# Retention and a squared-ReLU feed-forward on one core: q of the first four pairs read in 2 KB rows, and a new order on every engine

## The chip, the cores and the metric

The kernel runs on one core of a Trainium2 chip. Its time is the device time of one execution in microseconds; the time of a kernel is the median of its runs. Of one execution the profiler also left a trace: every instruction of TensorE (PE for matmuls, PEld for weight loads), VectorE (DVE), ScalarE (ACT) and GpSimd (POOL), the issues of SyncE (SP), and every packet of the 16 DMA engines.

## The reference

Eight batches, eight heads, 576 tokens, head dimension 64; then a feed-forward of 512 to 2048 to 512 over the 4608 tokens.

```python
def _attn_ref(q, k, v):
    scores = scale * np.matmul(q, k.transpose(0, 1, 3, 2))
    gamma = 1.0 - 2.0 ** (-5.0 - np.arange(H))
    rel = pos[:, None] - pos[None, :]
    Dmat = np.where(rel >= 0, gamma[:, None, None] ** rel[None, :, :], 0.0)
    return np.matmul(scores * Dmat[None], v)
...
    x = attn_out.transpose(0, 2, 1, 3).reshape(B * S, H * D)
    h = x @ w_in
    r = np.maximum(h, 0.0)
    return (r * r) @ w_out
```

## The kernel before

**Units, pairs, groups.** A unit is 128 tokens of one batch with all heads (36 in all; the last 64 tokens of two batches share a tail unit). Two units form a group g, 18 groups. The first eight units are loaded as four pairs of 256 tokens (`add_load_pair`, L308): k, q and v of a pair are one DMA of 512 KB each, with two neighbouring tokens of a head, 512 bytes, as a row. Later units are loaded one by one (`add_load`, L290), their q in 1 KB rows by four DMAs.

**Retention.** For a pair (`add_unit_pair`, L403), k and q are cast to fp16 into `kx` and `qx` (L424) on the engine that the code names (DVE, ACT or POOL), and v is scaled by its decay into `vx` (L420). TensorE transposes `kx` and `qx` (L439, into `psT`), and ACT or DVE evicts them to `kqT` (L450). Then (`add_ret_pair`, L468) come the scores `psc` (quarter-array matmuls, L357), the causal mask on DVE (L490, into `rx`), the sums `psS` of the state, the state update on DVE (L514, L461, into `R`), the outputs `psO`, and their product with `gam_full` on DVE, which writes the feed-forward's input `xT` (L577). Later units use DMA transposes (L400) and the lines L371, L382, L387, L692 and L751 in place of these.

**Feed-forward.** For each group (`add_ff`, L858), 64 matmuls `ph` (L876) multiply `xT` with `w_in`; ACT takes the ReLU into `rl` (L884), and ACT or DVE squares it into `gT` (L894, L896), eight times per group (fb 0 to 7). Group 0 multiplies `gT` by `w_out` directly (L916, 16 steps of two units). The other groups use one level of Strassen's scheme (`add_strassen`, L932): seven products of eight matmuls (L973) on sums `gS` that DVE makes (L946), and on sums `wT` of `w_out` that DVE makes once (L827). Product 6 needs the sum s2, which DVE makes in two halves of 128 x 512. ACT and DVE then assemble the output (L986, L996, L1047) and SP stores it (L845).

**Weights.** `w_in` and `w_out` are read by eight DMAs that POOL issues (L331) and that write fp16: w0 to w3 are quarters of `w_in`, w4 to w7 of `w_out`. w0 is issued when v of the first pair has landed. k of the third pair (k4) waits for w5.

**What sets the order.** Nothing is issued where the code stands. Every task goes to a small planner (`Schedule`, L16) with its engine, a priority (`key`), a planned duration, its dependencies and the buffers that it takes. `emit` plays the plan through and then issues the instructions engine by engine in that order. Each engine works in order, so the plan's durations and landing times decide what stands behind what. Warm-up matmuls (L256, `WARM` of them) have the lowest priority and fill TensorE while it has nothing else in the plan.

```python
        loaded[name, u] = loaded[name, u + 1] = dma_task(0, 1.81 if loaded else 2.9, fn, acq=("wst",) if name != "q" else (),
                                                         after=2.1 + LAG.get(name + str(u), 0.0))
```

Of the kernel before, what the change touches and what calls it, by code (L numbers as in the profile page):

```python
# [15 lines left out]
class Schedule:  # L16
# [6 lines left out]

    def add(self, eng, key, dur, fn, deps=(), acq=(), after=None, lag=0.0):
        t = dict(eng=eng, key=key, dur=dur, fn=fn, acq=acq, n=len(self.tasks), users=[], free=[], lag=lag,
                 left=len(deps), ready=0.0, lat=self.LAT[eng] if after is None else after)
        for d in deps:
            d["users"].append(t)
        self.tasks.append(t)
        return t  # L30
# [11 lines left out]
    def emit(self):  # L42
# [10 lines left out]
        for t in self.tasks:  # L53
            if t["left"] == 0:
                heapq.heappush(ready[t["eng"]], (t["key"], t["n"], t))
        now = 0.0
        while True:
            for e in ready:
# [3 lines left out]
                while ready[e]:  # L62
                    item = heapq.heappop(ready[e])
                    t = item[2]
                    if all(self.count[r] >= t["acq"].count(r) for r in t["acq"]):
                        for r in t["acq"]:
                            self.count[r] -= 1
                        t["start"] = now
                        order.append(t)
                        busy[e] = True  # L70
                        push(now + t["dur"], "end", t)
                        break
                    held.append(item)
# [5 lines left out]
            while events and events[0][0] <= now + 1e-9:  # L79
                _, _, what, t = heapq.heappop(events)  # L80
                if what == "end":
                    busy[t["eng"]] = False
                    for w in t["users"]:

                        push(now + (0.0 if w["eng"] == t["eng"] else t["lat"]), "dep", w)
# [18 lines left out]
def kernel(  # L104
# [105 lines left out]

    mask2 = const.tile([P, 2, 2, 64], FP32, name="mask2")
    nc.gpsimd.memset(mask2, 1.0)
    for c in range(2):
        for e in range(2):
            m = mask2[c * 64:(c + 1) * 64, e]
            nc.gpsimd.affine_select(out=m, in_=m, compare_op=ALU.is_ge, fill=0.0, base=-e, pattern=[[1, 2], [2, 64]],  # L216
                                    channel_multiplier=-2)
# [6 lines left out]
    L = 2 * NF  # L224
    WARM = 34
    EARLY = 20
    SQ_ACT = (0, 1, 2, 3, 4, 5, 6)
    SPREAD = 0.1
    QL = 0.8
    BESIDE = 1.1  # L230
    PAUSE = 1.5
# [4 lines left out]
    JOIN = 5  # L236
    LAG = {"k4": 0.7, "q4": 0.5}
    LAG_T, LAG_O = 1.5, 5.0
# [69 lines left out]
    def add_load_pair(name, u):  # L308
        n = "kqv".index(name)

        def fn():
# [3 lines left out]
            b, c = units[u][1:]  # L315
            t = nc.sync.dma_start(out=x, in_=(k, q, v)[n][b, :, c * P:(c + 2) * P, :].rearrange("h (p e) d -> p h (e d)", e=2))
            if (name, u) == ("k", 4):
                behind(t, tile_of["w", 5])
            tile_of["load", name, u] = t
        loaded[name, u] = loaded[name, u + 1] = dma_task(0, 1.81 if loaded else 2.9, fn, acq=("wst",) if name != "q" else (),  # L320
                                                         after=2.1 + LAG.get(name + str(u), 0.0))

    issues = []

    def add_weight(i):
# [9 lines left out]
        issues.append(issue)  # L335
        t = add("SP", 0, 2.75, lambda: None, deps=last_load + [issue], after=2.1 + LAG.get(f"w{i}", 0.0))
        last_load[:] = [t]
# [65 lines left out]
    def add_unit_pair(u, base):  # L403
# [4 lines left out]
        for i, name in enumerate("kqv"):  # L408
            xs[name] = []
            for e in range(2):  # L410
                eng = ("DVE" if (e if name == "v" else lead) else "ACT" if name == "k" and u >= 4 or u == 2 and e else
                       "DVE" if name == "q" and u == 2 else "POOL")

                def fc(name=name, e=e, eng=eng):
# [4 lines left out]
                    if name == "v":  # L419
                        (nc.vector if eng == "DVE" else nc.gpsimd).tensor_tensor(  # L420
                            out=t.rearrange("p (h d) -> p h d", d=D), in0=x,
                            in1=vdec[f"pair{e}"].rearrange("p (h o) -> p h o", o=1).to_broadcast([P, H, D]), op=ALU.mult)
                    else:
                        engines[eng](out=t.rearrange("p (n b a d) -> p n b a d", n=2, b=2, a=2),  # L424
# [9 lines left out]
        for i, name in enumerate("kq"):  # L434
# [9 lines left out]
            for s in range(2):  # L444
                on_act = i == 0 or s == 0 or u > 0

                def fe(i=i, s=s, on_act=on_act):
                    if i == 0:
                        tile_of["kqT", u + s] = work.tile([P, 2 * NP, P], FP16, name="kqT", tag="kqT", bufs=6)
                    (nc.scalar.copy if on_act else nc.vector.tensor_copy)(  # L450
                        out=tile_of["kqT", u + s][:, i * NP:(i + 1) * NP].rearrange("p x (e t) -> p e x t", e=2),
                        in_=tile_of["psT", u, i][:, :, :, half(s)])
                es.append(add("ACT" if on_act else "DVE", base + 3 + i + s / 2, 0.66, fe, deps=[t] + T["kqT", u + s],
# [14 lines left out]
    def add_ret_pair(g):  # L468
# [7 lines left out]
        for e in range(2):  # L476
# [11 lines left out]
            for a in range(2):  # L488
                def fm(e=e, a=a):
                    nc.vector.tensor_tensor(  # L490
                        out=rT[e][:, a], in0=rT["ps", e][a].rearrange("p (n i) -> p n i", i=P),
                        in1=mask2[:, e].rearrange("p (o e) i -> p o (e i)", o=1).to_broadcast([P, NP, P]), op=ALU.mult)
                ms.append(add("DVE", base + 5 + e, 0.66, fm, deps=[t] + ms))
# [79 lines left out]
        for s in range(2):  # L573
            def fx(s=s):
                if s == 0:
                    tile_of["x", g] = x_pool.tile([P, NP, 2 * P], FP16, name="xT", tag="xT")
                nc.vector.tensor_tensor(  # L577
                    out=tile_of["x", g][:, :, s * P:(s + 1) * P].rearrange("p n (i e) -> p n e i", e=2),
                    in0=tile_of["psO", g][s].rearrange("p (n e i) -> p n e i", n=NP, e=2),
                    in1=gam_f.rearrange("p n (i e) -> p n e i", e=2), op=ALU.mult)  # L580
            T["x", u + s] = add("DVE", base + 25 + s, 0.7, fx, deps=[t] + ([T["x", u]] if s else []), acq=() if s else ("x",))
# [119 lines left out]
    def after_sums(g, t, key, res):  # L701
# [23 lines left out]
        r1 = add("DVE", key + 0.2 - URGENT, 0.69, fr1, deps=[r0])  # L725
        r2 = add("DVE", key + 0.3, 0.65, fr2, deps=[r1], acq=("R",))
        T["Rm", g], T["R", g], T["Rread", g], T["Rmread", g] = r0, r2, [], r1
# [94 lines left out]
    def add_wT(i, in0, in1):  # L822
        ts = []
        for h in range(2):
            def f(h=h):
                sl = slice(h * HF // 2, (h + 1) * HF // 2)
                nc.vector.tensor_tensor(out=wT[i][:, sl], in0=in0[:, sl], in1=in1[:, sl], op=ALU.subtract)  # L827
            ts.append(add("DVE", WT_KEY + i, 0.7, f, deps=sum((wcast[j] for j in range(4, 8 if i else 6)), [])))
        return ts
# [5 lines left out]
    for x, y in ((t2, t1), (t4, t2)):  # L835
        for p in y:
            for w in x:
                sched.need(w, p)
    wT_done = {7: t3, 6: t2, 5: t1, 4: t4}
# [18 lines left out]
    def add_ff(g):  # L858
# [10 lines left out]
        for fb in range(NF // nf):  # L869
# [18 lines left out]
            def fg(fb=fb, on_act=on_act):  # L888
# [6 lines left out]
                else:  # L895
                    nc.vector.tensor_tensor(out=t, in0=rl, in1=rl, op=ALU.mult)  # L896
            r = add("ACT", place(4 * fb + 4), 0.6, fr, deps=[f1[-1]], acq=("rl",))
            sched.free("ff", [r])
            sq.append(add("ACT" if on_act else "DVE", place(4 * fb + 6), 0.63 if on_act else 0.55, fg, deps=[r] + sq[:1],
                          acq=() if fb else ("g",)))  # L900
            sched.free("rl", [sq[-1]])
# [30 lines left out]
    def add_strassen(g, us, base, sq):  # L932
# [7 lines left out]
        def add_sum(k, key, parts, in0, in1, op, deps, start=()):  # L940
            out_ = []
            for h in range(parts):
                def f(sl=cut(parts, h)):
                    if ("S", g) not in tile_of:
                        tile_of["S", g] = stage.tile([P, 4, HF, P], FP16, name="gS", tag="wst")
                    nc.vector.tensor_tensor(out=tile_of["S", g][:, k, sl], in0=in0(sl), in1=in1(sl), op=op)  # L946
                out_.append(add("DVE", key + h, (BESIDE if h else 0.5) if parts > 1 else 0.8, f, deps=deps(h, parts) + list(start)))
            sums[k] = out_
# [163 lines left out]
```

## Time and profile before

| | us |
|---|---|
| median of 4 runs | 290.83 |
| lowest and highest | 290.15, 292.28 |
| the profiled execution | 289.97 |
| its span | 288.3 |
| TensorE busy | 281.5 |
| ScalarE, VectorE, GpSimd busy | 187.4, 178.7, 86.6 |
| granted TensorE clock | 0.997 |

The profile's times count from the start of the span. Busy time of TensorE includes the warm-up matmuls, and a busy TensorE isn't TensorE at its peak, since matmuls are pipelined. A row of a group gives line, engine, operation, output and inputs, the shape, the count, and the mean time of one.

### The profile page before, as it was taken

Reading aid. Unit: us, or ns where it says so; the run is one execution under the profiler, and the core shown is the slowest. Engines: PE = TensorE matmul, PEld = TensorE weight load, DVE = VectorE, ACT = ScalarE, POOL = GpSimd, SP = SyncE. Lnnn points to the kernel's source line nnn. Section 1 sums busy time; section 2 is a strip of 40 time slices with the busy share of each in tenths; the row PEclk is TensorE's granted clock in tenths of the full one; section 3 lists DMA queues with packets and bytes.
Section 4 is the critical chain, followed back from the end, with each engine's and each line's share of the span. In section 5 each row is a group of like instructions: output and inputs, shape, how many; then the busy total and the mean of one; then the engine's idle time right before and its main releaser. Section 6 shows DMA issues by size and latency. Waiting matters only on the chain.

```text
span 288.3 us, 10135 instructions
## 1 busy us (share of the span) xinstructions
PE 281.5 (98%) x4346; PEld 236.5 (82%) x4346; DVE 178.7 (62%) x341; ACT 187.4 (65%) x363; POOL 86.6 (30%) x124
## 2 busy tenths in 40 slices
PE   7999999999999999999999999999999999999994
PEld 3568767888888888888888888888888888888883
DVE  3772379968466656747656664867665566364632
ACT  4558975667585857657575748675848675847830
POOL 5560035434435242423235151524423100000000
PEclk9999999999999999999999999999999999999998
DMA  7999999999998898989999897969898620102004
GB/s 197 277 208 206 246 280 268 173 241 152 196 229 175 216 201 212 173 209 175 213 172 234 196 211 170 240 161 251 184 158 211 116 77 2 73 2 75 0 4 144
DMA packets 122157, 49.94 MB, mean 173 GB/s; under 512 B 94721, under 2 KB 117761, under 8 KB 122113
## 3 DMA queue, kind: packets, MB, share of 16 engines
q1 hardware_dynamic: 117568, 44.84, 70.5%
q0 software_dynamic: 4224, 4.19, 8.8%
q8 instruction: 34, 0.56, 0.8%
q10 hardware_dynamic: 320, 0.26, 0.4%
q14 instruction: 11, 0.08, 0.1%
HBM read 36.70 MB, written 9.44 MB: 160 GB/s over the span
## 4 chain that ended last, share of the span: by engine, by line
PE 91%; DMA 3%; POOL 2%; issue 2%; DVE 0%; POOLq 0%; DVEq 0%
PE ph L876 44%; PE po L973 37%; PE psO L357 4%; DMA w_in<-in_moe_w_in_dram 3%; PE po L916 2%; PE psc L357 2%; PE psS L357 2%; PE psT L439 1%; POOL mask L216 0%; POOL vx L420 0%; POOL w_in L331 0%; DVE o L996 0%; POOL mask_full L208 0%; POOL mask_tail L208 0%; DVE p L1025 0%
## 5 line engine op out<-in xcount | busy, mean ns | idle before, releaser
L876 PE MATMUL ph<-xT,w_in 128*128 128x256 f16 x1152 | 136.5, 273 | 0.1
L876 PEld LDWEIGHTS <-w_in 128*128 128x128 f16 x1152 | 111.5, 98 | 14.4 <-DMA w_in<-in_moe_w_in_dram 0.4
L884 ACT ACTIVATE rl<-ph 128x512 f16<-128x512 f32 x144 | 84.3, 586 | 50.6 <-PE ph L876 48.0
L894 ACT ACTIVATE gT<-rl 128x512 f16<-128x512 f16 x118 | 74.4, 631 | 3.4
L973 PEld LDWEIGHTS <-gS 128*128 128x128 f16 x544 | 51.7, 98 | 6.5
L973 PE MATMUL po<-wT,gS 128*128 128x256 f16 x408 | 55.8, 273 | 0.0
L946 DVE TENSOR_TENSOR gS<-gT,gS 128x512 f16<-128x512 f16 (+1 forms) x51 | 30.0, 588 | 23.2 <-ACT gT L894 22.6
L973 PEld LDWEIGHTS <-gT 128*128 128x128 f16 x408 | 39.6, 98 | 4.8
L973 PE MATMUL po<-w_out,gT 128*128 128x256 f16 x272 | 36.7, 273 | 0.0
L387 POOL TENSOR_TENSOR v<-v,vdec_full 128x512 f16<-128x512 f32 x24 | 26.8, 1117 | 26.5 <-DMA v<-in_v_dram 17.6
L946 DVE TENSOR_TENSOR gS<-gT 128x1024 f16<-128x1024 f16 x34 | 26.2, 770 | 6.0 <-ACT gT L894 5.9
L371 POOL CAST kq<-k 128x512 f16<-128x512 f32 x28 | 19.5, 695 | 33.8 <-DMA k<-in_k_dram 29.5
L382 POOL CAST kq<-q 128x512 f16<-128x512 f32 x24 | 15.4, 641 | 36.1 <-DMA q<-in_q_dram 36.0
L896 DVE TENSOR_TENSOR gT<-rl 128x512 f16<-128x512 f16 x26 | 12.1, 466 | 20.5 <-ACT rl L884 20.5
L996 DVE TENSOR_TENSOR o<-po,u 128x256 f32<-128x256 f32 x33 | 13.9, 422 | 15.2 <-PE po L973 7.5
L986 ACT COPY u<-po 128x256 f32<-128x256 f32 x34 | 12.5, 368 | 15.7 <-PE po L973 15.6
L751 DVE TENSOR_TENSOR xT<-psO,gam_full 128x512 f16<-128x512 f32 x28 | 18.0, 684 | 3.8 <-PE psO L357 3.6
L996 DVE TENSOR_TENSOR o<-po,p 128x256 f32<-128x256 f32 x18 | 7.6, 424 | 20.2 <-ACT u L986 13.5
L973 PE MATMUL po<-w_out,gS 128*128 128x256 f16 x136 | 18.0, 273 | 0.0
L692 DVE TENSOR_TENSOR rT<-psc,mask_full 128x512 f16<-128x512 f32 x24 | 15.6, 685 | 3.7 <-PE psc L357 3.4
L973 PE MATMUL po<-wT,gT 128*128 128x256 f16 x136 | 17.6, 273 | 0.0
L461 DVE TENSOR_TENSOR R<-stmp,dec 128x512 f16<-128x512 f32 (+1 forms) x18 | 13.0, 722 | 0.5
(82 smaller groups left out, 221.7 us busy)
## 6 DMA issues: line engine op xcount, KB each, us to landing
out_dram<-o SPq DMA_DIRECT2D x32, 256.0 KB, 2.7
k<-in_k_dram SPq DMA_DIRECT2D x24, 256.0 KB, 4.3
q<-in_q_dram SPq DMA_DIRECT2D x96, 64.0 KB, 3.1
v<-in_v_dram SPq DMA_DIRECT2D x24, 256.0 KB, 3.9
pair<-in_k_dram SPq DMA_DIRECT2D x4, 512.0 KB, 6.3
pair<-in_q_dram SPq DMA_DIRECT2D x4, 512.0 KB, 6.7
pair<-in_v_dram SPq DMA_DIRECT2D x4, 512.0 KB, 7.7
w_in<-in_moe_w_in_dram POOLq DMA_DIRECT2D x4, 512.0 KB, 9.0
```

The costliest lines, as they stand in the source:

```text
L357: t = nc.tensor.matmul(out_, lhsT=lhsT, rhs=rhs, start=start, stop=True, skip_group_check=True, tile_position=(64 * row, 64 * col))
L371: op(out=out_.rearrange("p (n b a d) -> p n b a d", n=2, b=2, a=2), in_=in_.rearrange("p (a n b) d -> p n b a d", n=2, a=2))
L382: nc.gpsimd.tensor_copy(out=tile_of["kq", u][:, 1].rearrange("p (t a d) -> p a t d", t=4, a=2), in_=tile_of["q32", u].rearrange("p (a t) d ...
L387: nc.gpsimd.tensor_tensor(out=t, in0=tile_of["v32", u], in1=vdec[kind].rearrange("p (h o) -> p h o", o=1).to_broadcast([P, H, D]), op=ALU. ...
L692: tile_of["masking", g] = nc.vector.tensor_tensor(out=tile_of["rT", g][:, :, a], in0=tile_of["psc", g][a].rearrange("p (s n i) -> p s n i" ...
L751: nc.vector.tensor_tensor(out=tile_of["x", g].rearrange("p n (s e i) -> p e (n s) i", s=n, e=2)[:, c], in0=y.rearrange("p (o t r) -> p o r ...
L876: nc.tensor.matmul(tile_of["ph", g, fb][:, j, :], lhsT=w_in16[:, m, fi * P:(fi + 1) * P], rhs=tile_of["x", g][:, m, :], start=(m == 0), st ...
L884: nc.scalar.activation(out=t, in_=tile_of["ph", g, fb], func=ACTF.Relu)
L894: nc.scalar.activation(out=t, in_=rl, func=ACTF.Square)
L946: nc.vector.tensor_tensor(out=tile_of["S", g][:, k, sl], in0=in0(sl), in1=in1(sl), op=op)
L973: nc.tensor.matmul(tile_of["pb", g, bank], lhsT=left(i), rhs=right[:, i, :], start=(start and i == 0), stop=(i == HF - 1), skip_group_chec ...
L996: nc.vector.tensor_tensor(out=o_tile(u)[:, half * HM:(half + 1) * HM], in0=bank(x), in1=tile_of[name, g], op=ALU.add)
```

## The change

q of each of the four pairs is read by two DMAs, one for each half of the heads. A row is eight neighbouring tokens of one head, 2 KB, and the 128 partitions are 32 token groups by 4 heads. Tokens of q therefore lie in another order in `qx`, and the eviction of the transposed q (now in shape 8 x 4 x 16), the mask `mask2` and the product that writes `xT` are written for it. k and v stay as they are. The q and k casts of the second pair are both on ACT now.

The planner gets other durations for these loads and for the weights, other lags, fewer warm-up matmuls, and an account of the case that a DVE task marked `soft` runs while POOL is in a task of more than 0.5 us: then it proceeds at 0.22 of its speed. `soft` tasks are the squares, the sums `gS`, the sums `wT` and one state update. Their planned durations are shorter than before, and the allowance `BESIDE` of 1.1 for the second half of a split sum is gone. `HURRY` raises the priority of group 1's last ReLU, DVE squares and sums. The sums `wT` depend on the slices that they read, half by half.

With that, the order of instructions is another on TensorE, DVE, ACT and SP. On TensorE the matmuls of `ph` (L876) and the first products with `w_out` (L916) alternate as 28, 48, 4, 16, 4, 16, 4, 20, 12, where it was 28, 52, 4, 20, 4, 16, 4, 12, 20 (the 28 `ph` stand ahead of the second group's outputs). The two halves of product 6 follow each other without `ph` between them in five of the groups from 2 to 15; before, at least eight matmuls stood between them in all groups from 2 to 15.

```diff
@@ class Schedule
+    SHARED = 0.22
...
+        def shared(beside):
+            t = port["task"]
+            if t is not None:
+                port["left"] -= (now - port["at"]) * (self.SHARED if port["beside"] else 1.0)
+                port["at"] = now
+                t["end"] = now + max(port["left"], 0.0) / (self.SHARED if beside else 1.0)
+                push(t["end"], "end", t)
+            port["beside"] = beside
...
-    mask2 = const.tile([P, 2, 2, 64], FP32, name="mask2")
+    mask2 = const.tile([P, 2, 8, 16], FP32, name="mask2")
...
-    WARM = 34
+    WARM = 26
...
-    BESIDE = 1.1
+    HURRY = 60
...
-    LAG = {"k4": 0.7, "q4": 0.5}
+    LAG = {"k0": 0.3, "w7": 1.4, "v6": 1.2}
@@ add_load_pair
-            t = nc.sync.dma_start(out=x, in_=(k, q, v)[n][b, :, c * P:(c + 2) * P, :].rearrange("h (p e) d -> p h (e d)", e=2))
+            src = (k, q, v)[n][b, :, c * P:(c + 2) * P, :]
+            if name == "q":
+                for a in range(2):
+                    t = nc.sync.dma_start(out=x[:, NP * a:NP * a + NP].rearrange("p t d -> p (t d)"),
+                                          in_=src.rearrange("(a x) (r t) d -> a r x (t d)", a=2, t=8)[a])
+            else:
+                t = nc.sync.dma_start(out=x, in_=src.rearrange("h (p e) d -> p h (e d)", e=2))
...
-        loaded[name, u] = loaded[name, u + 1] = dma_task(0, 1.81 if loaded else 2.9, fn, acq=("wst",) if name != "q" else (),
+        loaded[name, u] = loaded[name, u + 1] = dma_task(0, 2.9 if not loaded else 1.41 if name == "q" else 1.81, fn, acq=("wst",) if name != "q" else (),
@@ add_weight
-        t = add("SP", 0, 2.75, lambda: None, deps=last_load + [issue], after=2.1 + LAG.get(f"w{i}", 0.0))
+        t = add("SP", 0, 2.58, lambda: None, deps=last_load + [issue], after=3.0 + LAG.get(f"w{i}", 0.0))
@@ add_unit_pair
-                eng = ("DVE" if (e if name == "v" else lead) else "ACT" if name == "k" and u >= 4 or u == 2 and e else
-                       "DVE" if name == "q" and u == 2 else "POOL")
+                eng = ("DVE" if (e if name == "v" else lead) else "ACT" if name == "k" and u >= 4 or u == 2 and name != "v" else "POOL")
...
+                    elif name == "q":
+                        x = tile_of["q32", u].rearrange("p (a t) (s d) -> p a (t s) d", a=2, s=2)[:, :, NP * e:NP * e + NP]
+                        engines[eng](out=t.rearrange("p (t a d) -> p a t d", t=NP, a=2), in_=x)
...
+                    else:
+                        out_ = out_.rearrange("p x (t r) -> p t x r", r=16)
+                        in_ = in_.rearrange("p e y (r x) -> p (e y) x r", x=NP)[:, :, :, 16 * s:16 * s + 16]
@@ add_ret_pair
-                    out=tile_of["x", g][:, :, s * P:(s + 1) * P].rearrange("p n (i e) -> p n e i", e=2),
-                    in0=tile_of["psO", g][s].rearrange("p (n e i) -> p n e i", n=NP, e=2),
-                    in1=gam_f.rearrange("p n (i e) -> p n e i", e=2), op=ALU.mult)
+                    out=tile_of["x", g][:, :, s * P:(s + 1) * P].rearrange("p n (r t) -> p n r t", t=8),
+                    in0=tile_of["psO", g][s].rearrange("p (n t r) -> p n r t", n=NP, t=8),
+                    in1=gam_f.rearrange("p n (r t) -> p n r t", t=8), op=ALU.mult)
@@ add_wT
-            ts.append(add("DVE", WT_KEY + i, 0.7, f, deps=sum((wcast[j] for j in range(4, 8 if i else 6)), [])))
+            ts.append(add("DVE", WT_KEY + i, 0.68, f, deps=wcast[4 + h] + (wcast[6 + h] if i else []), soft=True))
@@ add_ff, add_strassen
-            r = add("ACT", place(4 * fb + 4), 0.6, fr, deps=[f1[-1]], acq=("rl",))
+            r = add("ACT", place(4 * fb + 4) - HURRY * (g == 1 and fb == 7), 0.6, fr, deps=[f1[-1]], acq=("rl",))
...
-                out_.append(add("DVE", key + h, (BESIDE if h else 0.5) if parts > 1 else 0.8, f, deps=deps(h, parts) + list(start)))
+                out_.append(add("DVE", key + h - HURRY * (g == 1), 0.43 if parts > 1 else 0.72, f, deps=deps(h, parts) + list(start), soft=True))
```

## The prediction

> **What bounds the kernel now.** I read the page's busy times first, then the chain that ended last in order of time, then engine times by stretch, then the timeline of TensorE in the stretch that decides, and last the instructions on the tile that feeds TensorE in the steady part.
>
> ```profile
> PE 281.5 (98%) x4346; PEld 236.5 (82%) x4346; DVE 178.7 (62%) x341; ACT 187.4 (65%) x363; POOL 86.6 (30%) x124
> ...
> PE 91%; DMA 3%; POOL 2%; issue 2%; DVE 0%; POOLq 0%; DVEq 0%
> ```
>
> TensorE is busy nearly always and 91% of the chain is its own work. The rest is the start and the tail. The chain in order of time shows where TensorE last waited for data:
>
> ```profile
> 9.02 0.98 POOL w_in L331
> 10.07 0.99 POOL vx L420
> 11.07 8.64 DMA w_in<-in_moe_w_in_dram
> 19.75 1.48 PE ph L876 x12
> 22.32 5.78 PE ph L876 x52
> ```
>
> The second slice of w_in, issued at 11.07, lands at 19.71, and from there the chain is TensorE to 283.28. Engine times by stretch (PE, PEld, DVE, ACT, POOL, clock, DMA share, GB/s):
>
> ```profile
> 0.00:17.70 17.70, 15.70 (x234) 8.06 (x234) 11.26 (x51) 8.58 (x19) 11.87 (x32) 1.00 1.03 231
> 17.70:36.00 18.30, 18.11 (x197) 14.40 (x191) 7.38 (x14) 16.13 (x29) 1.70 (x3) 1.00 1.23 223
> ...
> 120.00:260.00 140.00, 139.87 (x2305) 122.32 (x2303) 87.27 (x151) 92.53 (x180) 38.76 (x49) 1.00 0.74 161
> ```
>
> Before 17.7 TensorE is filled with warm-up matmuls (11.0 us of L256). After it, it idles 0.2 us in 17.7:36 and 0.1 us in 120:260. So no reordering of the steady part can win anything there, it can only lose. What can be won is the time of the first stretch, and this is set by transfers:
>
> ```profile
> 10.00:12.00 2.00, 1.65 (x44) 0.86 (x39) 2.00 (x4) 0.62 (x1) 1.93 (x4) 1.00 1.20 290
> 14.00:16.00 2.00, 1.91 (x70) 1.25 (x58) 1.92 (x3) 1.02 (x3) 1.77 (x2) 1.00 1.23 208
> 30.00:32.00 2.00, 2.00 (x17) 1.41 (x15) 0.69 (x1) 1.97 (x4) 0.00 (x0) 1.00 1.25 206
> ```
>
> The DMA engines are full from 4 to 40 us: at 290 GB/s with the pairs' 512-byte rows, then at 206 GB/s with the weights. The weights are counted as the fp16 that is written; they read twice that, 412 GB/s, in 2 KB rows. TensorE uses each slice as it lands (timeline of TensorE):
>
> ```profile
> 17.73 3.50 PE L876 MATMUL ph<-xT,w_in 128*128 128x256 f16 x28
> 27.94 1.03 PE L916 MATMUL po<-w_out,gT 128*128 128x512 f16 x4
> 30.98 1.03 PE L916 MATMUL po<-w_out,gT 128*128 128x512 f16 x4
> 33.59 1.03 PE L916 MATMUL po<-w_out,gT 128*128 128x512 f16 x4
> 35.77 4.48 PE L916 MATMUL po<-w_out,gT 128*128 128x512 f16 x20
> ```
>
> By the trace the eight weight slices w0 to w7 land at 17.27, 19.70, 22.21, 25.06, 27.61, 30.72, 32.69 and 35.49. Three of the four L916 groups start within 0.35 us of their slice.
>
> **q in 2 KB rows.** A pair's 512 KB take 1.8 us now (q0 lands at 6.89, v0 at 8.71). No load in 2 KB rows to fp32 is in the trace, so I bound it. The least gain is nothing, at 290 GB/s. The most is the weights' 412 GB/s: 524 KB / 412 = 1.27 us, 0.54 less. A loss needs a slower row than 512 bytes, which no row shows. [...] The trace has 290 GB/s at DMA share 1.20 for 512-byte rows and 412 read at 1.25 for 2 KB ones, so I follow the rows and take 0.45 per q, 0.9 for the two ahead of the weights. Each q is now two issues on SP; a small issue at L298 costs 0.43 us, so v0 is issued near 2.4 instead of 1.95, while its data is not due before about 5.8. That costs nothing; without the transfers ahead of it, it would cost 0.45.
>
> **The weights.** POOL issues w0 at 9.01, 0.30 after v0 landed; v0 gains one q, 0.45. The end of the pair loads gains two, 0.9. The stream starts between the two; I take every weight slice 0.8 earlier (range 0 to 1.3): w0 16.5, w1 18.9, w4 26.8, w5 29.9, w6 31.9, w7 34.7. The cast of kx (0.62) leaves POOL, so w2's issue moves up too; the stream is in order and this brings nothing.
>
> **The first stretch.** For pair 2 ACT now does all four k and q casts (4 x 0.62 from about 10.1, the last pair from q2's landing at 11.4) and then four evictions (2.14), to about 14.8; it ended at 16.40. VectorE loses a qx cast (0.42): from the first mask near 10.0 it has four masks 2.56, state updates 1.25, vx 0.69, xT 1.36, so xT is ready at about 15.9 (16.05 now). The q eviction, the masks (0.68 each) and the xT products (0.68 each, now a strided read from PSUM and a dense write where it was the other way round) work on equally many elements in the new token order, so I keep their times; a strided read could add 0.2 to the one DVE eviction (0.42), at most that, and 0.2 to each xT, and both are covered up to w0's landing 0.6 after xT. So the first ph waits for w0, 16.5, and the seventeenth for w1, 18.9: TensorE is 0.8 ahead there.
>
> **Warm-up, 34 to 26 matmuls.** They are fillers. The clock is 1.00 in 0:17.7 with 15.70 of 17.70 busy. [...] The holes left by eight fillers (8 x 0.216) are split by transposes and scores, so I take 0 and keep 1.7 for the range.
>
> **What the new order gives back.** The L916 groups stand after 28+48, 16, 16 and 20 ph where they stood after 28+52, 20, 16 and 12. From ph 17 at 18.95 the second psO block is done at 21.4, 48 ph (0.109 each) end at 26.65: 0.2 wait for w4. Group (0.87) and 16 ph (1.75) end at 29.5: 0.4 wait for w5, so TensorE stands at 30.0 where it stood at 30.98, but with 8 fewer ph behind it, 0.87. Net 0.1. If w5 keeps the mean step of 2.60 (in this trace it took 3.11) the net is 0.5, and without any wait 0.8. I take 0.5.
>
> **36 to 52 us.** k4 is issued when w5 has landed, and q4 and q6 are shorter too, so these loads land 0.8 to 1.7 earlier; TensorE also asks earlier: 36.3 for k4, then q4 at 37.7 and two POOL casts (1.22) give 38.9, where TensorE comes at about 38.85. v4 at 39.45 plus POOL's vx (1.04 to 1.45) gives 40.5 to 40.9 against a need at 40.6. I take 0.1 of new waits, up to 0.6. DVE's wT subtractions now stand ahead of gT and sums and wait for w5 and w6; behind them are the squares and sums of group 1, which HURRY puts ahead of other work and which are needed after 41, so this is hidden; vx of the fifth unit stands behind them too and waits for v4 anyway. On SP two loads now stand ahead of the first stores; the stores wait up to 16.7 us as it is, unseen by TensorE.
>
> **Steady part and tail.** The matmuls are the same in number and shape, and after the last long run of ph TensorE's order is the same as now. TensorE's work there can't shrink, so I take nothing, except for rival A.
>
> **Sum.** The profiled execution took 289.97, 288.3 of it span. -0.5 and +0.1: 289.6. The median of the runs is 290.83, 0.86 above the profiled one; the same change there gives 290.4.
>
> **Rivals.** A, slower: the sums on VectorE come too late. The page of tile gS:
>
> ```profile
> L946 DVE TENSOR_TENSOR gS<-gT,gS x51: 415/484/1526, 35.0 to 274.7; 128x512 f16<-128x512 f16 x34, 128x1024 f16<-128x1024 f16 x17
> ```
>
> The same half takes 0.42 or, beside a POOL instruction, up to 1.53. The planner used to count the second half as 1.1 and 8 or more ph (0.87) stood between the two halves of product 6 in all of groups 2 to 15. Now it counts 0.43 and stretches it where it expects POOL, and in five groups nothing stands between them. The second half has been ready 0.6 to 1.8 us before its use; 0.87 less leaves 0.2 to 0.7, and a late POOL (it waits for k loads, 29.5 us in all at L371) costs the excess, up to 0.9 per group. It decides from about three such groups on: 5 x 0.5 gives +2.5, 292.1 by the profile, 292.9 by the median. Against it: 6 of 34 halves took over 0.6 us.
>
> [...]
>
> C, everything arrives at the upper bound: weights 1.3 earlier, no wait for w4 and w5, and the three drains of about 0.3 hidden: -1.6, 289.2.
>
> **How the numbers follow.** A measurement of this kernel tells about 0.5% (1.45 us) from no change. Forecast 0.5, A 0.2, B 0.15, C 0.15. Faster takes two thirds of C and a tenth of the forecast, 0.16; slower most of A, a part of B and the clock, and a twentieth of the forecast, 0.25; the rest, 0.59, is no change. The range goes from C's lower half to A, 288.9 to 292.9.
>
> **What would show it.** Right: q0 landing near 6.4, w1 near 18.9, the first ph near 16.5, L916 starting at 27 and 30, waits of 0.2 to 0.6 on w_in and w_out, and a steady part with under 0.3 us of idle TensorE. Wrong: w1 at 19.7 (B), idle TensorE before L973 released by DVE gS (A), a clock under 1.00 in the first 20 us, or a first ph before 15.5.

## The result, and the profile after

The changed kernel takes 291.75 us (median of 44 runs, 289.95 to 294.38) where the kernel before, run beside it, takes 290.42 us (63 runs). The ratio is 1.0039, with a 95% interval of 1.0024 to 1.0054. It is slower, by 1.1 us by the ratio and 1.3 by the medians. That is less than the 0.5% that I had put as the limit of a measurement; this many runs tell 0.15%. A second set of runs, later, gave 292.27 against 289.94 us, a ratio of 1.0074 (1.0048 to 1.0100, six runs of the changed kernel). The forecast was 0.4 us faster.

The profiled execution took 292.63 us, 290.9 of it span. From its page, the busy time of TensorE, the granted clock in 40 slices of 7.3 us, and the shares of the chain:

```profile
PE 279.9 (96%) x4338; PEld 235.8 (81%) x4338; DVE 175.6 (60%) x340; ACT 188.8 (65%) x365; POOL 86.2 (30%) x123
...
PEclk9979999999999999999999999999999999999999
...
PE 84%; ACT 3%; DVE 3%; DMA 2%; SPq 2%; POOL 2%; issue 1%; POOLq 0%; DVEq 0%
```

The span is 2.6 us longer and TensorE is busy 1.6 us less, and the third slice has a clock of 7 tenths. Two things went wrong, then: TensorE was slow once, and it stood still. Engine times by stretch say where (columns: length, then busy time of PE, PEld, DVE, ACT, POOL, the clock, DMA share, GB/s):

```profile
0.00:17.70 17.70, 13.02 (x228) 7.11 (x229) 11.28 (x48) 9.41 (x21) 11.90 (x32) 1.00 1.00 239
16.00:18.00 2.00, 1.26 (x62) 0.95 (x51) 2.00 (x4) 0.00 (x0) 2.00 (x4) 0.93 1.25 205
18.00:20.00 2.00, 2.00 (x11) 1.34 (x10) 1.97 (x5) 0.60 (x1) 0.61 (x1) 0.50 1.24 207
17.70:36.00 18.30, 18.20 (x179) 14.14 (x178) 8.84 (x16) 14.87 (x26) 0.91 (x2) 0.91 1.22 232
120.00:260.00 140.00, 138.25 (x2290) 120.71 (x2288) 85.63 (x150) 92.21 (x179) 40.47 (x49) 1.00 0.75 163
```

TensorE was busy 15.70 us in the first stretch and is busy 13.02 now: eight warm-ups fewer, and holes. The clock's records have it at 0.50 from 17.70 to 21.12. And in the steady part 1.75 us are idle where it was 0.13. The timeline of TensorE around the first `ph` and around the second hole:

```profile
15.81 0.41 PE L390 MATMUL psS<-vx,kx 64*64 64x64 f16 x28 [0.61 <-DVE vx L452]
16.03 0.61 PE L390 MATMUL psc<-kqT 64*64 64x128 f16 x29
17.38 0.25 PE L390 MATMUL psc<-kqT 64*64 64x128 f16 x3 [0.74 <-issue]
17.56 4.90 PE L914 MATMUL ph<-xT,w_in 128*128 128x256 f16 x28
28.73 1.03 PE L954 MATMUL po<-w_out,gT 128*128 128x512 f16 x4
...
122.41 0.30 PE L390 MATMUL psc<-kqT 64*64 64x64 f16 x16
124.36 0.32 PE L390 MATMUL psc<-kqT 64*64 64x64 f16 x16 [1.65 <-DMA kqT<-kq]
```

28 `ph` took 4.90 us where 28 took 3.50. At 122.41 the scores `psc` of group 9 begin, and their second unit waits until its transposed k and q land at 124.32. (From the last matmul's start at 122.52 to the next at 124.36 is 1.84 us; the row's 1.65 is less because it ends matmuls by a model. Waits below are given from start to start.) The chain of waits, asked for this window, shows what that transpose was late for:

```profile
108.49 1.04 DVE gS L984 x2
109.53 0.46 SPq L883
...
113.05 1.66 SPq L325
...
115.70 2.45 DMA q<-in_q_dram
...
118.36 1.14 POOL kq L415
119.50 0.02 issue
119.52 4.80 DMA kqT<-kq
124.32 0.04 issue
124.36 0.32 PE psc L390 x16
```

It is a chain without slack from the issue of q's load on SP over the cast on POOL to the DMA transpose, and it begins at a store (L883). The rows of SP and TensorE for the same group, first before, then after:

```profile
106.88 1.00 SPq L845 DMA_DIRECT2D out_dram<-o  x2
111.83 2.76 SPq L298 DMA_DIRECT2D q<-in_q_dram  x4
119.12 1.41 SPq L400 DMA_TRANSPOSE kqT<-kq  x1
124.78 0.43 PE L357 MATMUL psc<-kqT 64*64 64x64 f16 x32
```

```profile
107.86 2.13 SPq L883 DMA_DIRECT2D out_dram<-o  x2
113.05 3.08 SPq L325 DMA_DIRECT2D q<-in_q_dram  x4
119.52 2.46 SPq L433 DMA_TRANSPOSE kqT<-kq  x1
```

In the profile before, the second unit's scores began at 124.90 while its `kqT` had landed at 122.69: 2.2 us of slack. Now TensorE is ready for them 2.4 us sooner, at 122.52, and the `kqT` lands 1.6 us later, at 124.32. Together they make the wait. By the chain, the load is late because it stands behind the store on SP: that took 2.13 us in place of 1.00, as it waited for VectorE until 109.53.

### The profile page after: what moved, and what is told of

The parts are those of the page before. It is cut to its first block, busy times and chain, and to the rows that moved or that the text cites. A ratio compares the mean times of both kernels' runs of the same rounds, so it can differ in the third digit from the quotient of the medians.

```text
span 290.9 us, 10126 instructions
## 1 busy us (share of the span) xinstructions
PE 279.9 (96%) x4338; PEld 235.8 (81%) x4338; DVE 175.6 (60%) x340; ACT 188.8 (65%) x365; POOL 86.2 (30%) x123
## 4 chain that ended last, share of the span: by engine, by line
PE 84%; ACT 3%; DVE 3%; DMA 2%; SPq 2%; POOL 2%; issue 1%; POOLq 0%; DVEq 0%
PE ph L914 40%; PE po L1011 33%; PE psO L390 4%; PE po L954 2%; PE psc L390 2%; PE psS L390 2%; DMA kqT<-kq 2%; ACT rl L922 1%; SPq L325 1%; ACT gT L932 1%; PE psT L474 1%; DMA q<-in_q_dram 1%; DVE rx L529 1%; ACT kqT L491 1%; DVE R L500 1%
## 5 line engine op out<-in xcount | busy, mean ns | idle before, releaser
L914 PE MATMUL ph<-xT,w_in 128*128 128x256 f16 x1152 | 138.1, 275 | 0.0
L1011 PE MATMUL po<-wT,gS 128*128 128x256 f16 x408 | 55.0, 273 | 0.0
L984 DVE TENSOR_TENSOR gS<-gT 128x1024 f16<-128x1024 f16 x34 | 24.7, 726 | 7.2 <-ACT gT L932 6.5
L404 POOL CAST kq<-k 128x512 f16<-128x512 f32 x28 | 18.8, 671 | 32.3 <-DMA k<-in_k_dram 29.7
L415 POOL CAST kq<-q 128x512 f16<-128x512 f32 x24 | 15.9, 664 | 40.9 <-DMA q<-in_q_dram 40.7
L1011 PE MATMUL po<-wT,gT 128*128 128x256 f16 x136 | 17.6, 273 | 0.0
L500 DVE TENSOR_TENSOR R<-stmp,dec 128x512 f16<-128x512 f32 (+1 forms) x18 | 12.2, 679 | 0.5
```

What stands on the lines that cost most here:

```text
L404: op(out=out_.rearrange("p (n b a d) -> p n b a d", n=2, b=2, a=2), in_=in_.rearrange("p (a n b) d -> p n b a d", n=2, a=2))
L415: nc.gpsimd.tensor_copy(out=tile_of["kq", u][:, 1].rearrange("p (t a d) -> p a t d", t=4, a=2), in_=tile_of["q32", u].rearrange("p (a t) d ...
L914: nc.tensor.matmul(tile_of["ph", g, fb][:, j, :], lhsT=w_in16[:, m, fi * P:(fi + 1) * P], rhs=tile_of["x", g][:, m, :], start=(m == 0), st ...
L1011: nc.tensor.matmul(tile_of["pb", g, bank], lhsT=left(i), rhs=right[:, i, :], start=(start and i == 0), stop=(i == HF - 1), skip_group_chec ...
```

## The experiments

Four theories. **Theory 1:** the new order of the steady part asks for the scores of groups 6, 7 and 9 about 2 us earlier, while their loads come no sooner (the DMA share in 80:120 is 0.97 in the profiles before and after), so TensorE waits for them. **Theory 2:** with eight warm-ups fewer, the start has holes, and the clock is at 0.50 from 17.70 to 21.12 because of them. **Theory 3** (formed after the first four runs): the changed start is early at 26 us, but asks for the third pair at 40 us before it is there. **Theory 4:** the rows themselves cost time. The sums `gS` (rival A of the prediction) were out already, since the page puts only 0.2 us of the idle time before their weight loads down to them:

```profile
L1011 PEld LDWEIGHTS <-gS 128*128 128x128 f16 x544 | 51.9, 98 | 6.8 <-DVE gS L984 0.2
```

All results, as medians beside the kernel before on the same chip:

| run | us | before | ratio | 95% interval |
|---|---|---|---|---|
| load_alone | 289.95 | 289.86 | 1.0002 | 0.9989 to 1.0016 |
| order_alone | 291.74 | 289.86 | 1.0065 | 1.0044 to 1.0086 |
| more_warm | 290.48 | 289.86 | 1.0020 | 1.0010 to 1.0030 |
| start_after_rest_before | 290.47 | 289.86 | 1.0020 | 1.0008 to 1.0031 |
| more_warm_rest_before | 290.40 | 289.83 | 1.0013 | 1.0004 to 1.0021 |
| rows_start_before_rest_after | 291.14 | 289.83 | 1.0042 | 1.0031 to 1.0054 |
| more_warm_relief | 290.67 | 289.83 | 1.0025 | 1.0014 to 1.0037 |
| load_alone_26warm | 290.14 | 289.83 | 1.0011 | 0.9994 to 1.0029 |
| steady_after_relief | 289.74 | 289.92 | 0.9991 | 0.9973 to 1.0010 |
| load_alone_relief | 289.45 | 289.92 | 0.9990 | 0.9976 to 1.0005 |
| states_later | 290.10 | 289.92 | 1.0004 | 0.9993 to 1.0015 |
| rows_30warm | 289.62 | 289.92 | 0.9990 | 0.9976 to 1.0003 |
| after_again | 292.27 | 289.94 | 1.0074 | 1.0048 to 1.0100 |
| after_relief | 290.39 | 289.94 | 1.0014 | 1.0004 to 1.0024 |
| rows_30warm_again | 289.57 | 289.94 | 0.9985 | 0.9968 to 1.0002 |

In most of these the planner's run is replaced by a written list of task numbers, so that one part of an order can be kept while another is exchanged:

```diff
     def emit(self):
-        ... (the planner plays its plan and sorts the tasks by it)
+        for n in [int(n) for n in ORDER.split()]:
+            self.tasks[n]["fn"]()
```

### The load and the order apart

`load_alone` is before's order and warm-ups with the new q loads and layout:

```diff
-            t = nc.sync.dma_start(out=x, in_=(k, q, v)[n][...].rearrange("h (p e) d -> p h (e d)", e=2))
+            if name == "q":
+                for a in range(2):
+                    t = nc.sync.dma_start(out=x[:, NP * a:NP * a + NP]..., in_=src.rearrange("(a x) (r t) d -> a r x (t d)", a=2, t=8)[a])
```

> The kernel before, in its own order and with its 34 warm-ups, with only the q loads (two DMAs of 2 KB rows) and the layout that follows from them. Theory 1 (the new order asks for the scores of the next groups 1.5 to 2.5 us earlier, in a stretch where the loads land just in time): the rows cost nothing, same time as before, 290.0 to 290.8 us, and at most 0.4 us better. Theory 2 (eight fewer warm-ups let the TensorE clock drop to 0.50 for 3.4 us): likewise 290.0 to 290.8, clock 1.00. Theory 4 (the rows themselves cost time: q0's second half landed at 7.02 against 6.89 us, and the strided evictions of kqT on VectorE took 0.68 instead of 0.42 us): 291 to 292, as in the changed kernel.

`order_alone` is the opposite: the changed kernel's order and its 26 warm-ups, with before's q loads and layout (the same lines the other way round).

> The changed kernel's order of all engines and its 26 warm-ups, with the q loads and the layout of before. Theory 1: as slow as the changed kernel, 291.3 to 292.0 us, with a wait of 1 us or more of the scores for a kqT transpose between 80 and 140 us. Theory 2: also 291.3 to 292.0, with a stretch at clock 0.50 in the first 22 us of its profile. Theory 4: back to before's 290.4.

The load alone changes nothing (1.0002), so theory 4 is out, and the order alone is as slow as the whole change or slower (1.0065). Its profile has the wait of group 9 again, 1.04 us at 122.96, but no clock under 1.00 before 260 us, where theory 2 had expected one in the first 22 (one of its six runs had a mean clock of 0.994).

The load does bring something, only not to the end. In `load_alone` the eight weight slices land 1.0 to 1.9 us earlier than in the profile before (w1 at 18.67 for 19.70), and the second transpose of group 9 is issued by 118.01 for 120.53. But TensorE's first `ph` is at 17.97, no earlier than before's 17.73: `psS` starts 0.3 us later than before, and the four warm-ups behind it are run whatever has landed:

```profile
16.05 0.44 PE L363 MATMUL psS<-vx,kx 64*64 64x64 f16 x32
16.43 1.04 PE L256 MATMUL warm<-wT 128*128 128x512 f16 x4
17.40 0.64 PE L363 MATMUL psc<-kqT 64*64 64x128 f16 x32
```

### The steady order

`start_after_rest_before` takes the changed kernel up to group 1's last product (52 us) and before's order from there; `rows_start_before_rest_after` is its mirror image, with the new loads and 34 warm-ups:

```diff
-ORDER = after
+ORDER = after[:last product of group 1] + [n for n in before if not yet in]
```

> The changed kernel (its loads, its layout, 26 warm-ups) with its own order up to the last product of the second group (about 52 us) and from there the order of before on every engine. Theory 1: 289.9 to 290.8 us where the clock stays at 1.00, up to 1.7 more where it drops at 17 us; no wait of the scores over 1 us between 80 and 140 us. Theory 2: no better than the changed kernel, 291.3 to 292.0. Theory 4: 291.3 to 292.0.

> The loads and layout of the changed kernel, the order of before with its 34 warm-ups up to the last product of the second group (about 52 us), and from there the changed kernel's order. Theory 1 (the steady order asks for the scores of groups 6, 7 and 9 too early for their loads): 1.0012 to 1.0025, with the second kqT of these groups used less than 2.6 us after its transpose was issued and waits of up to 2 us there. Rival: the steady order costs only because the changed start leaves the loads late, so 1.0000 to 1.0006 here.

The first halves the loss (1.0020), the second, with before's good start, has all of it (1.0042, more than theory 1's 1.0012 to 1.0025). So the steady order costs by itself. The waits of TensorE for data in the second one's profile from 60 to 140 us (us in total, times, longest), and from SP's timeline the issue of group 9's second transpose:

```profile
PE psc L367 <- DMA kqT<-kq: 0.6, 2, 0.4
```

```profile
118.02 1.67 SPq L410 DMA_TRANSPOSE kqT<-kq  x1
```

The two waits are 0.43 us at group 7 and 0.55 at group 9.

To see whether it is the loads, they were made faster, with nothing else moved. k and v of the later units are read as rows of 256 bytes; in the relieved kernels they are rows of 2 KB, as many DMAs and bytes:

```diff
-                    nc.sync.dma_start(out=x, in_=src[b, :, c * P:(c + 1) * P, :].rearrange("h p d -> p h d"))
+                    nc.sync.dma_start(out=x.rearrange("p h d -> p (h d)"),
+                                      in_=src[b].rearrange("h s d -> (h s d)")[c * P * H * D:(c + 1) * P * H * D].rearrange("(p n) -> p n", p=P))
```

> The kernel with before's start and the changed kernel's order from 52 us on (1.0042 so far, with two waits of 0.43 and 0.55 us of the scores for kqT in its profile), with k and v of the single units from unit 8 on read as 2 KB rows from another place of the same tensor, so the numbers computed are others. Theory 1 (the steady order asks for scores sooner than the loads come): the second kqT of groups 6, 7 and 9 is issued more than 6 us ahead of its use, the waits are gone, and the time comes to 1.0000 to 1.0012. Rival (the new steady order costs 1 us for a reason other than loads): 1.003 or more.

> Control for the kernel with relieved loads: before's order throughout with the new q loads (1.0002 so far), and the same 2 KB rows of k and v from unit 8 on, from another place of the same tensor, so the numbers computed are others. In before's order no score waits for a load, so all theories expect 0.9990 to 1.0008; if it is outside of that, the relief does more than bring loads sooner, and the other run is to be read against this one.

With the edit the second kernel goes from 1.0042 to 0.9991, and the control in before's order from 1.0002 to 0.9990. The relief itself is therefore worth about 0.1%, and the remaining 0.4%, 1.1 us, was waiting for loads (known to about 0.3%, from the four intervals taken as independent). In the relieved profile the same transpose is issued at 111.64, 6.4 us sooner, and the scores at 121.46 wait for nothing. Theory 1 is shown for the steady order. The relief brings both the issues on SP and the transfers forward, so which of the two was short is not shown. One TensorE time says the same: from the 321st to the 705th `ph`, in the same order, it takes 89.03 us without relief and 87.86 with it.

### The start: warm-ups and the clock

`more_warm` puts the eight missing warm-ups into the holes of the changed start; every other instruction keeps its place. `load_alone_26warm` takes the last eight out of before's order.

```diff
-    WARM = 26
+    WARM = 34
```

> The changed kernel with all its instructions in its own order, and eight more warm-ups (34, as before) put in the idle gaps of its first 18 us. Theory 2: the clock stays at 1.00, and the time comes back to 290.2 to 290.7 us. Theory 1: the clock stays at 1.00 but only 0.3 to 0.6 us come back, 291.1 to 291.5. Theory 4: as theory 1.

> The kernel before with the new q loads and its own order, with the last eight of its 34 warm-ups taken out and nothing put in their place. Theory 2 (the warm-ups hold the clock): a share of the runs has the clock at 0.50 for 3.4 us in the first 22 us, 1.0015 to 1.003. Rival (the clock drop belongs to the gaps that the new order of the start leaves, not to the number of warm-ups): 1.0000 to 1.0006, clock 1.00 in the profile.

`more_warm` comes back half way (1.0020), with the clock at 1.00. Its 290.48 us lie in theory 2's range, but the kernel before was faster on this chip, and by the ratio it is between the two theories' forecasts. Its profile also has no wait for loads in the steady part, so the half that came back is not the clock's alone. `load_alone_26warm` is inconclusive as a ratio (1.0011, interval across 1), but its runs tell more. Sixteen of 22 had a mean clock of 0.997 or more and a median of 289.4 us, 0.5 below `load_alone`; six had 0.990 to 0.994 and a median of 291.8. A drop to 0.50 for 3.41 us, as in the changed kernel's profile, makes a mean of 0.994 in a span of 290 (1 - 0.5 x 3.41 / 290), so this is the size of such a drop; where in the run it fell is not on record. The groups are 2.4 us apart, more than the 1.7 us that 3.41 us at 0.50 come to (0.5 x 3.41, an estimate), so one such drop alone does not account for it. Why so little comes of the removed warm-ups is in the timeline (of a run of 290.81 us, one of the slower ones with a full clock):

```profile
15.64 0.41 PE L367 MATMUL psS<-vx,kx 64*64 64x64 f16 x28 [0.33 <-DVE vx L430]
15.87 0.85 PE L367 MATMUL psc<-kqT 64*64 64x128 f16 x29
17.43 0.25 PE L367 MATMUL psc<-kqT 64*64 64x128 f16 x3 [0.72 <-issue]
```

1.7 us of warm-ups are gone, but TensorE then waits for `vx`, and once for nothing that the profile shows, until 17.4. Every profile with 26 or 30 warm-ups has that wait (0.26 to 1.07 us by its rows). In the changed kernel's profile it ends at 17.38, and a 16 KB transfer of instructions has ended at 16.04; whether the one has to do with the other was not tried. The first `ph` comes at 17.6 in place of 17.97.

### The start: what it gives back

`more_warm_rest_before` joins the two good halves: the changed start with 34 warm-ups, before's order after 52 us.

> The loads and layout of the changed kernel, its own order with 34 warm-ups (eight more, in its gaps) up to the last product of the second group (about 52 us), and from there the order of before. The runs so far give, as ratios to the kernel before: loads alone 1.0002, all with 34 warm-ups 1.0020, changed start and before's rest 1.0020, all of the change 1.0039. If the eight missing warm-ups and the order of the steady part are two costs of half a microsecond each that add (theories 1 and 2 both), this one is at 1.0000 to 1.0006. If the order of the start costs by itself, whatever the clock does: 1.001 to 1.002.

1.0013, in the range of the second forecast: the start's order costs by itself. (The intervals of the two halves reach this far, so it is not clearly better than they are.) In its profile the 65th `ph` is at 25.88 (26.19 before), so the start does bring 0.3 us; but the 129th is at 52.30 (51.84 before). The timeline of TensorE shows one place where the gain goes:

```profile
39.21 1.46 PE L933 MATMUL po<-w_out,gT 128*128 128x512 f16 x6
41.06 0.45 PE L369 MATMUL psS<-vx,kx 64*64 64x64 f16 x32 [0.40 <-POOL vx L431]
```

`psS` of the third pair waits for POOL's `vx`, and that for v4, which lands behind all weights (at 39.87, w7 at 35.30, in the changed kernel's profile). `states_later` moves this one task back in TensorE's queue, behind five tasks that take about 1 us:

```diff
-... 557 psS(pair 3) 558 559 599 600 601 602 ...
+... 557 558 559 599 600 601 psS(pair 3) 602 ...
```

> The changed kernel with 34 warm-ups in its own start and before's rest (1.0013 so far), with one edit: TensorE's state sums of the third pair (psS from vx and kx) stand five products later in its queue, about 1 us, at 41 instead of 40 us. Theory 3 (the changed start is 0.3 us early at 26 us, but then asks for the third pair at 40 us before its cast of v, which follows a load that stands behind all weights, so the gain is given back in a wait of 0.4 to 0.55 us): the wait goes, 0.9992 to 1.0006. Rival (the loss between 26 and 52 us lies elsewhere, or the wait only moves to the next one behind): 1.0010 to 1.0018.

1.0004, as theory 3 had it, and the wait is not in its profile any more (that of its slowest run, 291.78 us). The interval (0.9993 to 1.0015) touches that of the run without the edit, so theory 3 is supported rather than settled.

`more_warm_relief` is `more_warm` with the relieved loads:

> The changed kernel with 34 warm-ups (1.0020 so far), and k and v of the single units from unit 8 on read as 2 KB rows in place of 256-byte rows, with as many DMAs and bytes; they are read from another place of the same tensor, so the numbers computed are others. Theory 1 (the scores of groups 6, 7 and 9 wait for loads that come just in time): the loads run ahead, the waits go, and the time comes to 1.0000 to 1.0006. Rival (the steady order costs for another reason, such as VectorE's sums or the order on TensorE): it stays at 1.0015 to 1.0025, however early the loads are.

This one missed: 1.0025, no gain from faster loads. The profile of `more_warm` has no wait for a load after 60 us either (`kqT` of groups 6 and 9 land 0.4 and 0.2 us ahead of use), so there was nothing to relieve; its loss is the start's. That it stands a little above `more_warm_rest_before` is within both intervals, and is left open.

### The changed kernel itself

> The changed kernel itself once more, for a second profile beside the first and a ratio on the chip of the other runs (1.0039 so far). If both causes are at work in it as a rule (the scores of group 6, 7 or 9 waiting for their loads, and the clock at 0.50 near 18 us), this profile shows one or both again; 1.003 to 1.0055. If the wait of 1.84 us at group 9 was an accident of the first profile, none of the three groups has its second kqT landing within 0.3 us of its use here.

> The changed kernel, order and 26 warm-ups as they are, with k and v of the single units from unit 8 on read as 2 KB rows from another place of the same tensor, so the numbers computed are others. Theory 1: what the late loads cost is gone, and what is left is the start's share (the run with the changed start and before's rest had 1.0020): 1.0005 to 1.0022. If the loads are not what the changed kernel loses to, 1.003 to 1.005.

The second profile of the changed kernel shows both again (and its ratio, 1.0074, is above the forecast): clock 0.50 from 17.67 to 21.08, and a wait of 1.21 us at group 9. With relieved loads and nothing else changed (the same edit as above):

```profile
18.00:20.00 2.00, 2.00 (x12) 1.42 (x10) 1.97 (x5) 0.85 (x2) 0.08 (x1) 0.50 1.24 206
...
120.00:260.00 140.00, 139.90 (x2307) 122.35 (x2306) 87.44 (x152) 92.47 (x180) 36.82 (x45) 1.00 0.62 149
```

The clock still drops, the steady part is full again, and the time goes from 292.27 to 290.39 (1.0074 to 1.0014). In the profiles the 705th `ph` is at 180.31 before, 182.95 in the changed kernel and 181.04 with relief: of the 2.64 us, 1.91 are waits for loads and 0.73 the start. The start's share includes the clock: in `after_relief` the five runs with a mean clock of 0.994 or less have a median of 291.16, the other 17 of 290.32, so the runs with such a clock are 0.8 us slower, less than the estimate of 1.7 from the drop's length; a later TensorE does not wait for the third pair (in the changed kernel's profile its `psS` starts at 41.87, with no wait). But `more_warm_relief`, the same order and loads with 34 warm-ups and a full clock in all its 13 runs, is not faster (1.0025), so with the loads out of the way the eight warm-ups bring nothing that these runs can tell. In the first 44 runs of the changed kernel 16 had such a clock; their median is 291.93, that of the others 291.76, so beside the scatter of the waits the drop is hardly seen.

### A version that uses the rows

`rows_30warm` is before's order with the new loads, less the last four warm-ups (run twice):

```diff
-    WARM = 34
+    WARM = 30
```

> Before's order with the new q loads and the last four of the 34 warm-ups taken out (with 34 it is at 1.0002; with 26 it had 11 of 22 runs at 289.0 to 289.7 us, some 0.5 us under those with 34, and 11 runs at 290.6 us and more). If the rows bring 0.4 us that 34 warm-ups hide, and four of the eight suffice to hold the clock: 0.9980 to 0.9995. If the first ph can't be earlier than 17.4 us anyway (the issue gap that ends there in all profiles with 26 warm-ups), or the clock still drops in part of the runs: 0.9996 to 1.0015.

> Before's order with the new q loads and 30 warm-ups once more, to narrow its ratio (0.9990, interval 0.9976 to 1.0003): 0.9980 to 0.9997 if the rows bring 0.3 us or more once some warm-ups make room for it; 0.9997 to 1.0010 if the first result was chance.

0.9990 and 0.9985. Each interval reaches past 1; their mean is 0.9988, and with half-widths of 0.00135 and 0.0017 taken as independent it is known to 0.0011: 0.35 us faster than before, and barely apart from no change. It beats the changed kernel clearly. The second profile took 292.61 us, the longest of its runs, and shows theory 1 in before's own order. TensorE's timeline, and then its engine times by stretch:

```profile
137.58 0.32 PE L367 MATMUL psc<-kqT 64*64 64x64 f16 x16 [1.69 <-DMA kqT<-kq]
```

```profile
138.01:141.43 3.42, 3.42 (x18) 2.45 (x17) 1.82 (x3) 1.33 (x3) 1.13 (x1) 0.50 0.86 252
```

TensorE was 0.9 us ahead of `load_alone` at 52 us (the 129th `ph` at 51.13), ran into the loads at group 10, and behind the hole the clock was at 0.50 from 138.01 to 141.43. Its transpose was also issued late, by 135.36 where `load_alone` had it by 130.69; why is not known.

## Why the prediction was wrong, point by point

**"TensorE's work there can't shrink, so I take nothing" (steady part).** This step failed, and it is most of the miss. The sentence before it was right: an order of a full TensorE can only lose. But I looked for the loss in VectorE's sums alone, and never compared the time at which each group's scores are asked for with the landing of its `kqT`. The profile before had the numbers: `kqT` of the second unit lands 1.4 us ahead of its use at group 8, 2.2 at group 9 and 0.04 at group 10, with a DMA share of 0.97 in 80:120. The new order asks 1.5 to 2.4 us sooner at groups 6, 7 and 9. Measured: 1.1 us after before's start (1.0042 to 0.9991, less 0.1% for the relief), 1.9 us in the profiles of the changed kernel.

**"The holes left by eight fillers (8 x 0.216) are split by transposes and scores, so I take 0 and keep 1.7 for the range."** Failed. The 0 was my estimate, and no run shows the 1.7. In their place the runs showed the clock at 0.50 for 3.41 us in three of the five profiles that have the changed start with 26 warm-ups (not in `order_alone` and `start_after_rest_before`), a sign of being wrong that the prediction itself names. By the medians, the runs with a mean clock of 0.994 or less are 0.2 us slower in the changed kernel (16 of 44) and 0.8 in `after_relief` (5 of 22). The holes are short: the wait just before the drop is 0.74 us by its row in the changed kernel, 1.01 in `after_again` and 1.07 in `after_relief`. The "clock is 1.00 in 0:17.7" was misread as well. The first clock record of that profile is at 6.87, and before 5.5 us its warm-ups start 0.43 us apart, half the pace of the later ones (0.22).

**"First ph at 16.5."** 17.56. w0 landed at 17.09 (in `load_alone` at 15.54), but the weights were not the last to come: `psc` stood until 17.38 in the issue gap. The fillers removed were mostly replaced by idle time.

**"0.45 per q" and "weights 0.8 earlier".** Of the right size, with more scatter than I gave it. q4 took 1.81 us before, 1.53 in the changed profile (36.75 to 38.28) and 1.36 in `load_alone` (35.86 to 37.22), so 0.28 and 0.45; the first q gained nothing in the changed profile, its second half landing at 7.02 for 6.89. The weights came 0.2 to 1.0 us earlier there, 1.0 to 1.9 in `load_alone`. The least that I had allowed was 0, at 290 GB/s; the runs reach from that to my 0.45. But transfers that land earlier were not the bound of TensorE, so this made no difference to the end.

**"I take 0.5" (new order) and "+0.1" (36 to 52 us).** The first two groups at L916 start at 27.16 and 29.77 in `more_warm`, just where I had them, with a gain of 0.3 at 26 us. The second term was mis-sized: I had v4's `vx` needed at 40.6 and ready at 40.5 to 40.9; it was needed at 40.6 and came at 41.0, and with the other small waits the stretch took 0.8 us more (26.44 from the 65th to the 129th `ph` for 25.65).

**Rival A**, VectorE's sums, was not it: 0.2 us. Rival B, that the rows bring no load sooner, had the right sign for a wrong reason, since they do: the weight slices by 0.2 to 1.0 us in the changed profile. The cause of most of the loss, loads against scores, was in none of the cases.

## What to carry to other kernels

When an order changes, list for every load of the steady part when it lands and when it is first needed, before and after: a slack of 2 us is a limit on how far the consumer may be moved ahead, and moving the consumer doesn't move the load. Take the slack from more than one profile: with the new q loads and before's order in the steady part, the issue of group 9's second transpose ended anywhere from 117.88 to 121.18. Take filler work out only where the work behind it is ready; otherwise the filler becomes idle time, and with it the clock was at 0.50 for 3.41 us in three of five profiles here. Two costs of a change need not add: a late start hides waits that an early start would meet (0.40 us for the third pair here), so exchange halves of the order both ways.

## What the runs showed of the hardware

In the changed kernel's profile the clock's records have 1.00 from 4.05 us, 0.50 from 17.70 to 21.12, and 1.00 after that until TensorE's work has ended; in the profile before they have 1.00 from 6.87 until then. TensorE's busy time in the changed kernel in the stretch of the drop and in one as long ahead of it:

```profile
14.29:17.70 3.41, 1.98 (x102) 1.49 (x91) 3.41 (x6) 0.95 (x2) 3.41 (x5) 1.00 1.24 206
17.70:21.12 3.42, 3.42 (x18) 2.36 (x17) 3.16 (x7) 1.25 (x3) 0.91 (x2) 0.50 1.26 211
```

In the 3.41 us ahead of the other drops TensorE was busy 1.67 us (`after_again`), 1.59 (`after_relief`) and 1.72 (`rows_30warm_again`). But in `order_alone` it was busy 1.59 us in 14.29:17.70 as well, and the clock stayed at 1.00. What makes the clock fall is not shown by these runs.

The wait of 1.84 us at group 9 in the first profile had no lower clock behind it (1.00 in 120:260). Behind the one of 1.88 us in `rows_30warm_again` the clock was at 0.50 from 138.01 to 141.43.

k and v of the later units in rows of 2 KB in place of 256 bytes brought the second transpose of group 9 forward from 121.98 to 113.32 and that of group 14 from 185.05 to 174.93 (ends of issue, the changed kernel without and with relief); the DMA share in 120:260 fell from 0.75 to 0.62. The strided eviction of `kqT` on VectorE took 0.68 us where the one before took 0.42, so 0.26 more where I had allowed an estimate of 0.2 at most; it cost nothing that reached the end (`load_alone`, 1.0002).
